# Two loads of the next batch's V, moved into an earlier chunk

## The chip, the cores and the metric

The kernel runs on one core of a Trainium2 chip. The metric is the time of one execution on the device in microseconds (us), as the median of several runs. Where a stretch of the run is meant, the times are from the first instruction of one profiled execution.

## What is computed

Eight batches of 3136 tokens. For each, scores of all tokens against all tokens from `z` (64 wide), a squared ReLU in place of a softmax, a sum over `v` (256 wide), and a product with `u`. Then 128 tokens of each batch, chosen by a gate, go through a two-layer network and replace their rows.

```python
scores = (1.0 / S) * np.matmul(z, z.transpose(0, 2, 1))
attn = np.maximum(scores, 0.0) ** 2
x = (u * np.matmul(attn, v)).astype(np.float32)
...
top_idx = np.argpartition(-s[b], capacity)[:capacity]      # s = x . w_gate
h = np.maximum(x[b, top_idx] @ w1, 0.0)
out[b, top_idx] = x[b, top_idx] + g[:, None] * (h @ w2)    # g = sigmoid(s[b, top_idx])
```

## The kernel before

Every matmul operand is kept as a high and a low part, and a product is made of three: high with high, high with low, low with high. In the profile `hi` and `lo` are the two parts of the squared scores, made by ACT (a cast) and by DVE or POOL (a subtraction).

A batch is worked through in seven chunks of columns: five of 512 (0 to 4), one of 256 (chunk 5) and one of 320 (chunk 6). A chunk has 13 slots: twelve with a pair of 128-row tiles of V each, and a last one for the 64 rows that are left. A slot is 12 matmuls into the chunk's two accumulator banks (line 561; in the last slot 4). A batch has 91 slots, and `k0` is the first slot of a batch.

The scores are symmetric. Where a chunk meets rows whose scores an earlier chunk has made, it doesn't compute them: the earlier chunk has transposed its squares (`aT`) and stored them to DRAM (`squares`, `squares_narrow`, `squares_last`), and `fetch` (line 382) brings them back into a buffer `qk`, of which there are three. Such slots are called old. In chunk 5 ten of twelve pairs are old, in chunk 6 eleven; one fetch serves two slots. For these, ACT makes `hi` from `qk` (line 423) and DVE or POOL makes `lo` (line 523). The work on scores runs `LEAD`, three, slots ahead of the matmuls that use it.

V of a batch comes from DRAM in thirteen steps. `stage_v` (line 284) loads four tiles of V (512 KB) into a buffer `vst` with four DMAs of 128 KB (line 293); there are two such buffers, which loads of weights and of stored squares (`fetch_own`, line 406) use too. `prep_v` (line 299) splits two of these tiles into high and low parts, on ACT (line 125) and POOL (line 126), into the buffers of V that the batch before leaves free in its last chunk.

When a chunk's last matmul is done, `finish` (line 600) multiplies its two banks with `u` on DVE (`ut`, line 607), which empties them. There are three banks for accumulators, so the next chunk's first bank is free at once and its second is free when the first `ut` is done. The first slot of a chunk works through its first bank, six matmuls, before it turns to the second (line 555).

All DMAs around here are issued by SP, one after the other in program order: fetches, loads of V, z and u, stores of squares and of the output (`out<-x`, line 626). Where one must wait for data or for a free buffer, all behind it wait.

The order is written out slot by slot. `plan` holds for each slot what is called ahead of its matmuls, in the order of the calls of `at_slot`. A fetch is planned `AHEAD`, seven, slots before its first use or as soon as a buffer is free (line 1352). `prep_v` for pair `g` stands at slot `k = k0 - 10 + 3 * g // 2` (line 1330), and the load of pairs `g` and `g + 1` three slots before it (line 1334). Loads are entered after the fetches (line 1366), so within a slot a fetch goes first. Stores that a slot's work has left go out after the next slot's matmuls are issued (line 1504).

Chunk 5 begins at slot `k0 - 26` and chunk 6 at slot `k0 - 13`. The first fetch for chunk 6 is so planned at slot 6 of chunk 5, the second at slot 9, and the first load of the next batch's V at slot 0 of chunk 6.

Of the kernel before, what the change touches and what calls it, by code (L numbers as in the profile page):

```python
# [88 lines left out]
def attention_then_routed_ffn(ctx: ExitStack, tc: tile.TileContext, zt, ut, v, wg, w1, w2, cst, cst16, keys, outs, at, cap):  # L89
# [141 lines left out]
    def stage_z(b, i, n=None, step=None, queues=(nc.sync, nc.sync)):  # L231
        a, w = part(i)
        n = n or w
        if n > CH or n != w:
            st = work.tile([P, CH // Q, GT * Q], F32, name="qk", tag="qk", bufs=NQ).rearrange("p f k -> p (f k)")
        else:
            st = stage.tile([P, CH], F32, name="zst", tag="zst", bufs=1)
        for h in range(2):
            queues[h].dma_start(st[h * 64 : h * 64 + 64, : step or n], zt[b, :, a : a + (step or n)])
        staged["z", b, i] = st  # L240

    def more_z(b, i, of):

        a, n = part(i)
        o = a - part(of)[0]
        for h in range(2):
            nc.sync.dma_start(staged["z", b, of][h * 64 : h * 64 + 64, o : o + n], zt[b, :, a : a + n])

    def prep_z(b, i, of=None, on=None, hi_on=None):

        of = i if of is None else of
        a, n = part(i)
        o = a - part(of)[0]
        m = min(n, NJ * P - a)
        src = staged["z", b, of][:, o : o + m].rearrange("p (f t a) -> p f t a", f=GT, a=Q)
        on = on or (nc.gpsimd.tensor_tensor if b else None)
        split(src, by_rows(ZH, a, m), by_rows(ZL, a, m), hi_on, lo_on=on)
        if m < n:
            split(staged["z", b, of][:, o + m : o + n], ZH[:, a + m : a + n], ZL[:, a + m : a + n], lo_on=on)
        spend(pool=0.65 + 0.0017 * n if b else 0.0)  # L260

    def bring_z(b, c):

        c0, w = CHUNKS[c]
        t = const.tile([P, CH], F32R, name="Z", tag="Z", bufs=2)[:, within(c)]
        for rows, z in ((slice(0, 64), ZH), (slice(64, P), ZL)):
            if b == 0 and c == 0:
                st = staged["z", 0, 0][rows]
                if z is ZH:
                    nc.scalar.copy(t[rows], st)  # L270
                else:
                    by_token = [x.rearrange("p (f t a) -> p f t a", t=GT, a=Q) for x in (t[rows], st)]
                    nc.vector.tensor_tensor(*by_token, by_rows(ZH, 0, CH)[rows].bitcast(F32), op=ALU.subtract)
            else:
                m = min(w, NJ * P - c0)
                nc.scalar.copy(
                    t[rows, :m].rearrange("p (f t a) -> p f t a", f=GT, a=Q), by_rows(z, c0, m)[rows].bitcast(F32)
                )
                if m < w:
                    nc.scalar.copy(t[rows, m:], z[rows, c0 + m : c0 + w].bitcast(F32))  # L280
                spend(act=0.1 + 0.001 * w)
        Z[b, c] = t

    def stage_v(b, g, queues=(nc.sync,) * GT):

        st = stage.tile([P, GT, D], F32, name="vst", tag="vst")
        if g < NJ // GT:
            tiles = GT if g < WHOLE else GT // 2
            for t in range(0, GT, tiles):
                for f in range(GT):  # L290
                    t0 = g * CH + t * P + f * tiles * Q
                    src = v[b, t0 : t0 + tiles * Q, :].rearrange("(t a) d -> a t d", a=Q)
                    queues[f].dma_start(st[f * Q : (f + 1) * Q, t : t + tiles], src)
        else:
            for h in range(2):
                nc.sync.dma_start(st[h * 64 : h * 64 + 64, 0, :], v[b, NJ * P :, :])
        staged["v", b, g] = st

    def prep_v(b, g, on=None):

        st = staged["v", b, g // 2][:, g % 2 * 2 :]
        n = 2 if 2 * g < NJ else 1
        if n == 2:
            t = vpool.tile([P, 2, NK, 2 * P], F32R, name="V", tag="V")
        else:
            t = vpool.tile([P, 2, NK, P], F32R, name="Vr", tag="Vr", bufs=1)
        src = st[:, :n].rearrange("p a d -> p (a d)").rearrange("p (f h i) -> p h f i", h=NK, i=Q)
        parts_of = [t[:, w].rearrange("p h (f i) -> p h f i", i=Q) for w in range(2)]
        lo_on, took = on or nc.gpsimd, {"dve": 1.0} if on else {"act": 0.6, "pool": 1.3}
        if not on and b == 0 and n == 2 and busy["pool"] + 1.3 > busy["dve"] + 0.6:  # L310
            lo_on, took = nc.vector, {"act": 0.6, "dve": 0.6}
        split(src, *parts_of, on and on.tensor_copy, lo_on.tensor_tensor)
        for q in range(n):
            V[b, 2 * g + q] = t[:, :, :, q * P : (q + 1) * P]
        spend(**took)
# [278 lines left out]
    def load_u(b, c):  # L594
        c0, w = CHUNKS[c]
        t = tail.tile([P, NK, CH], F32, name="ut", tag="ut", bufs=1)
        nc.sync.dma_start(t[:, :, :w], ut[b, :, :, c0 : c0 + w].rearrange("h p t -> p h t"))
        chunk[b, c] = t
# [700 lines left out]
    def at_slot(k, fn, act=0.0, dve=0.0):  # L1299
        if k < len(slots):  # L1300
            plan.setdefault(max(k, 0), []).append((fn, act, dve))

    def at_slots(k, load, use, act, dve=0.0, lead=2):

        at_slot(k, use, act, dve)
        loads.append((k - lead, load))
# [3 lines left out]
    for b in range(B):  # L1310
        k0 = b * per

        for i in range(NCH):
            if b == 0:
                k = (0, 0, 0, 1, 3, 5, 6)[i]
            elif i < WHOLE:
                k = k0 - per + (i + 1) * SLOTS + 7
            else:
                k = k0 - 1 + 4 * (i - WHOLE)
            use = lambda b=b, i=i: prep_z(b, i)  # L1320
            if b:
                at_slots(k, lambda b=b, i=i: stage_z(b, i), use, 0.6, lead=5 if i < WHOLE else 2)
            elif i > 2:
                at_slot(k, lambda i=i: prep_z(0, i, 1 if i < WHOLE else WHOLE), 0.6, 0.7)
                if i == WHOLE:
                    loads.append((2, lambda: stage_z(0, WHOLE, S + 64 - WHOLE * CH)))
                elif 3 < i < WHOLE:
                    loads.append((max(1, k - 3), lambda i=i: more_z(0, i, 1)))
        for g in range(NJ // 2 + 1):
            k = k0 - 10 + 3 * g // 2 if b else max(1, g - 3)  # L1330
            if b or g > 3:
                at_slot(k, lambda b=b, g=g: prep_v(b, g))
            if (b or g > 6) and g % 2 == 0:
                load = (k - (3 if b else 2), lambda b=b, g=g: stage_v(b, g // 2))
                if b or 2 * g < NJ:
                    loads.append(load)
                else:
                    at_slot(*load)
        for c in range(NCH):
            if b or c:  # L1340
                at_slot(k0 + c * SLOTS - LEAD - 4, lambda b=b, c=c: bring_z(b, c))
        for c in range(NCH):
            at_slot(k0 + c * SLOTS + 7, lambda b=b, c=c: load_u(b, c))
# [7 lines left out]
    for (b, c, g), ks in used.items():  # L1351
        k = max(ks[0] - AHEAD, room.popleft() - LEAD + 2)
# [6 lines left out]
    for i, (load, use) in enumerate(weight_tasks):  # L1359
        c, step = ((1, 11), (2, 4), (2, 10), (3, 4), (3, 10), (4, 4), (NCH + 1, 4), (NCH + 2, 4))[i]  # L1360
        k = c * SLOTS + step
# [232 lines left out]
```

## Time and profile before

| | |
|---|---|
| median of 3 runs | 2063.77 us (2062.52 to 2064.70) |
| the profiled execution | 2064.51 us, its span 2062.7 us |
| TensorE matmuls (PE) busy | 2046.9 us |
| VectorE (DVE) busy | 1531.1 us |
| POOL (GpSimd) busy | 1356.5 us |
| ScalarE (ACT) busy | 1291.0 us |
| granted clock of TensorE | 1.00 of full speed in the stretches looked at |
| moved by DMA | 415.52 MB, mean 201 GB/s |

Idle time of an engine is listed with what ended it; TensorE's is the one that makes the run longer. The ends of matmuls are modelled in the profile, so the distance between the starts of two matmuls tells more than the end of one. In a timeline a row merges like instructions that follow each other (x4), and brackets hold the idle time of the engine before it and what ended that.

### The profile page before, as it was taken

What the parts mean: (1) busy time and instruction counts of PE and PEld (TensorE: products, weight loads), DVE (VectorE), ACT (ScalarE), POOL (GpSimd) and SP (SyncE); (2) the same over time, 40 slices, a digit from 0 to 9 for tenths busy, and PEclk for the clock granted to TensorE, in tenths of its full rate; (3) what the DMA queues carried; (4) which work ended last, traced back from release to release, by engine and by line L of the source; (5) the groups of instructions that cost most, each with busy time, mean ns of one, the idle gap of its engine ahead of it and who ended that gap; (6) DMA issues with size and microseconds to landing.
All of it is one profiled execution on the core that took longest, in us unless ns stands there. A gap on an engine that the chain in (4) does not pass through costs nothing.

```text
span 2062.7 us, 31660 instructions
## 1 busy us (share of the span) xinstructions
PE 2046.9 (99%) x10280; PEld 1735.4 (84%) x10280; DVE 1531.1 (74%) x2667; ACT 1291.0 (63%) x1629; POOL 1356.5 (66%) x728
## 2 busy tenths in 40 slices
PE   9999999999999999999999999999999999999999
PEld 6888988889888898888988889888898888888788
DVE  7676678856788667875678757887578876787776
ACT  7665577655775467664676546765477655775543
POOL 6766587655876568764677647875578755665653
PEclk9999999999999999999999999999999999999999
DMA  6788767886668875787767877678676786666862
GB/s 198 209 235 227 212 188 207 238 227 187 197 185 232 214 209 176 198 237 206 207 184 194 237 202 218 183 194 239 191 222 187 193 197 182 206 190 164 216 173 95
DMA packets 442758, 415.52 MB, mean 201 GB/s; under 512 B 133792, under 2 KB 374880, under 8 KB 439520
## 3 DMA queue, kind: packets, MB, share of 16 engines
q1 hardware_dynamic: 441456, 411.01, 70.8%
q0 software_dynamic: 768, 2.10, 0.3%
q8 instruction: 80, 1.31, 0.3%
q14 instruction: 86, 0.70, 0.1%
q10 hardware_dynamic: 368, 0.39, 0.1%
HBM read 238.78 MB, written 174.60 MB: 200 GB/s over the span
## 4 chain that ended last, share of the span: by engine, by line
PE 78%; DVE 8%; DMA 4%; issue 3%; ACT 3%; SPq 2%; POOL 2%; POOLq 0%; DVEq 0%; ACTq 0%
PE acc L561 65%; PE sc L445 11%; DVE aT L488 2%; DVE a L467 2%; DMA qk<-squares_narrow 1%; DMA squares<-aT 1%; POOL lo L523 1%; ACT a L455 1%; ACT hi L456 1%; DVE lo L523 1%; PE h L1223 1%; PE y L1267 1%; DMA vst<-in_v 1%; DVE base L773 0%; DVE ut L607 0%
## 5 line engine op out<-in xcount | busy, mean ns | idle before, releaser
L561 PE MATMUL acc<-hi,V 128*128 128x512 f32 (+2 forms) x5376 | 1213.2, 364 | 4.8 <-DVE ut L607 2.3
L523 POOL TENSOR_TENSOR lo<-a,hi 128x1024 fp32r<-128x1024 f32 (+2 forms) x326 | 719.4, 2209 | 556.4 <-DVE a L467 443.0
L561 PEld LDWEIGHTS acc<-hi,V 128*128 128x128 f32 x5376 | 928.3, 188 | 162.4 <-DVE ut L607 8.4
L561 PE MATMUL acc<-lo,V 128*128 128x512 f32 (+2 forms) x2688 | 661.5, 362 | 1.5 <-POOL lo L523 1.4
L455 ACT ACTIVATE a<-sc 128x1024 f32<-128x1024 f32 (+4 forms) x401 | 358.5, 894 | 444.3 <-PE sc L445 419.4
L561 PEld LDWEIGHTS acc<-lo,V 128*128 128x128 f32 x2688 | 468.7, 188 | 77.8 <-POOL lo L523 4.5
L467 DVE TENSOR_TENSOR a<-sc,a 128x1024 f32<-128x1024 f32 (+5 forms) x306 | 307.5, 1005 | 244.3 <-ACT hi L456 220.0
L423 ACT CAST hi<-qk 128x1024 fp32r<-128x1024 f32 (+2 forms) x327 | 279.0, 860 | 223.0 <-PE acc L561 188.5
L488 DVE STREAM_TRANSPOSE aT<-a 128x512 f32<-128x512 f32 (+3 forms) x541 | 349.6, 681 | 75.5 <-ACT a L461 55.1
L456 ACT ACTIVATE hi<-a 128x1024 fp32r<-128x1024 f32 (+4 forms) x401 | 372.3, 928 | 24.7 <-PE acc L561 2.2
L523 DVE TENSOR_TENSOR lo<-qk,hi 128x1024 fp32r<-128x1024 f32 (+2 forms) x220 | 321.8, 1473 | 85.1 <-ACT hi L423 83.1
L445 PE MATMUL sc<-Z,ZH 128*128 128x512 f32 (+2 forms) x746 | 274.3, 372 | 2.5 <-DVE a L467 2.1
L445 PE MATMUL sc<-Z,ZL 128*128 128x512 f32 (+2 forms) x746 | 273.1, 370 | 0.0
L523 POOL TENSOR_TENSOR lo<-qk,hi 128x1024 fp32r<-128x1024 f32 (+2 forms) x107 | 209.5, 1960 | 50.2 <-ACT hi L423 41.1
L445 PEld LDWEIGHTS sc<-Z,ZH 128*128 128x128 f32 x746 | 140.0, 188 | 31.9 <-DVE a L467 6.0
L445 PEld LDWEIGHTS sc<-Z,ZL 128*128 128x128 f32 x746 | 140.1, 188 | 24.8 <-DVE ZL L126 0.4
L126 POOL TENSOR_TENSOR V<-vst,V 128x512 fp32r<-128x512 f32 x92 | 137.1, 1496 | 30.3 <-ACT V L125 27.2
L628 POOL TENSOR_TENSOR ut<-x,w_run 128x1024 f32<-128x1024 f32 (+2 forms) x52 | 125.6, 2416 | 30.3 <-DVE x L619 29.3
L461 ACT ACTIVATE a<-a 128x1024 f32<-128x1024 f32 x93 | 98.8, 1062 | 2.9
L126 POOL TENSOR_TENSOR ZL<-zst,ZH 128x512 fp32r<-128x512 f32 (+2 forms) x56 | 83.5, 1496 | 2.4 <-ACT ZH L125 2.1
L125 ACT CAST V<-vst 128x512 fp32r<-128x512 f32 x95 | 57.9, 609 | 36.6 <-DMA vst<-in_v 36.6
L607 DVE SCALAR_TENSOR_TENSOR ut<-acc,ut 128x512 f32<-128x512 f32 (+2 forms) x112 | 63.9, 612 | 19.5 <-PE acc L561 19.2
(187 smaller groups left out, 1081.2 us busy)
## 6 DMA issues: line engine op xcount, KB each, us to landing
squares<-aT SPq DMA_DIRECT2D x160, 512.0 KB
qk<-squares SPq DMA_DIRECT2D x320, 256.0 KB
squares_narrow<-aT SPq DMA_DIRECT2D x320, 128.0 KB
qk<-squares_narrow SPq DMA_DIRECT2D x80, 512.0 KB
out<-x SPq DMA_DIRECT2D x162, 128.0 KB
ut<-in_ut SPq DMA_DIRECT2D x40, 512.0 KB
vst<-in_v SPq DMA_DIRECT2D x158, 128.0 KB
squares_own<-aT SPq DMA_DIRECT2D x39, 256.0 KB
```

The source lines that it names most:

```text
L126: (lo_on or nc.vector.tensor_tensor)(lo, src, hi.bitcast(F32), op=ALU.subtract)
L423: nc.scalar.copy(by(hi), src)
L445: nc.tensor.matmul(ps[:, q], z[:, j * P : (j + 1) * P], mov, start=z is ZH, stop=z is ZL)
L455: nc.scalar.activation(a, ps[:, :n], AF.Relu)
L456: nc.scalar.activation(pieces[0][0](hi), pieces[0][1], AF.Square)
L461: nc.scalar.activation(a, a, AF.Square)
L467: square = lambda: nc.vector.tensor_tensor(a[rows], of[rows, :n], a[rows], op=ALU.mult)
L488: nc.vector.transpose(to, a[rows, q].rearrange("p (m t a) -> p m t a", m=GT, a=Q))
L523: on.tensor_tensor(view(lo), src, view(hi).bitcast(F32), op=ALU.subtract)
L561: nc.tensor.matmul(ac[h], w, mov, start=first and h not in started, stop=stop)
L607: nc.vector.scalar_tensor_tensor(xT[:, h, :w], acc[b, c][h], SCALE * SCALE, xT[:, h, :w], op0=ALU.mult, op1=ALU.mult)
L628: nc.gpsimd.tensor_tensor(wx, runs, consts["wg_run"].rearrange("p (o r) -> p o r", o=1).broadcast_to([P, NB, RUN]), op=ALU.mult,)
```

## The change

In the plan of V's loads, for every batch but the first, the load of pairs 0 and 1 moves from slot `k0 - 13` to `k0 - 22`, and that of pairs 2 and 3 from `k0 - 10` to `k0 - 17`. These are slots 4 and 9 of the 256-column chunk, nine and seven slots sooner. All other loads keep their slots (`13 - 3 * g // 2` is the old distance), and `prep_v` keeps its own.

```diff
-                load = (k - (3 if b else 2), lambda b=b, g=g: stage_v(b, g // 2))
+                load = (k0 - {0: 22, 2: 17}.get(g, 13 - 3 * g // 2) if b else k - 2, lambda b=b, g=g: stage_v(b, g // 2))
```

## Rows read from the trace of the kernel before

**Rows 1.** The page, part 1: busy us (share of the span), instructions.

```profile
PE 2046.9 (99%) x10280; PEld 1735.4 (84%) x10280; DVE 1531.1 (74%) x2667; ACT 1291.0 (63%) x1629; POOL 1356.5 (66%) x728
```

**Rows 2.** Waits of PE, whole run: us in total, times, longest us.

```profile
PE acc L561 <- DVE ut L607: 2.3, 5, 0.6
PE acc L561 <- ACT hi L423: 2.1, 2, 1.2
```

**Rows 3.** Waits of all engines, whole run: ACT's for loads of V.

```profile
ACT V L125 <- DMA vst<-in_v: 36.6, 21, 4.9
```

**Rows 4.** Stretches, seams 1, 2, 4: length, busy us by engine, clock, DMA share, GB/s.

```profile
233.24:258.66 25.42, 24.84 (x164) 24.07 (x163) 17.24 (x22) 17.49 (x27) 14.79 (x10) 1.00 0.76 211
488.33:514.91 26.58, 25.39 (x164) 24.13 (x163) 15.74 (x21) 17.16 (x26) 15.14 (x10) 1.00 0.72 196
...
997.13:1023.34 26.21, 25.31 (x164) 24.13 (x163) 15.79 (x21) 17.36 (x26) 15.19 (x10) 1.00 0.72 201
```

**Rows 5.** Timeline of PE, first slot of chunk 6, seams 1 and 2: start, length.

```profile
233.82 0.45 PE L561 MATMUL acc<-lo,V 128*128 128x320 f32 x2
234.85 0.86 PE L561 MATMUL acc<-hi,V 128*128 128x320 f32 x4 [0.58 <-DVE ut L607]
...
488.91 0.45 PE L561 MATMUL acc<-lo,V 128*128 128x320 f32 x2
489.20 0.84 PE L561 MATMUL acc<-hi,V 128*128 128x320 f32 x4
```

**Rows 6.** Timeline of ACT around seams 1, 2 and 4.

```profile
232.02 1.35 ACT L423 CAST hi<-qk 128x640 fp32r<-128x640 f32 x2 [1.90 <-DVE aT L488]
...
238.99 0.73 ACT L423 CAST hi<-qk 128x640 fp32r<-128x640 f32 x1 [1.06 <-PE acc L561]
...
486.33 0.73 ACT L423 CAST hi<-qk 128x640 fp32r<-128x640 f32 x1 [1.12 <-DMA qk<-squares_narrow]
...
498.98 0.62 ACT L125 CAST V<-vst 128x512 fp32r<-128x512 f32 x1 [4.92 <-DMA vst<-in_v]
...
995.15 0.73 ACT L423 CAST hi<-qk 128x640 fp32r<-128x640 f32 x1 [1.14 <-DMA qk<-squares_narrow]
```

**Rows 7.** Timeline of DVE at seam 1, around the chunk's finishing step.

```profile
232.78 1.56 DVE L523 TENSOR_TENSOR lo<-qk,hi 128x640 fp32r<-128x640 f32 x2 [0.78 <-ACT hi L423]
234.37 0.76 DVE L607 SCALAR_TENSOR_TENSOR ut<-acc,ut 128x256 f32<-128x256 f32 x2
```

**Rows 8.** Timeline of SP's issues, seam 1; the last row is seam 2.

```profile
223.14 0.52 SPq L399 DMA_DIRECT2D qk<-squares_narrow  x1
223.76 2.73 SPq L626 DMA_DIRECT2D out<-x  x4
226.59 1.15 SPq L399 DMA_DIRECT2D qk<-squares_narrow  x1
227.79 0.52 SPq L402 DMA_DIRECT2D qk<-squares_narrow  x1
...
229.35 0.49 SPq L402 DMA_DIRECT2D qk<-squares_narrow  x1
232.03 0.80 SPq L503 DMA_DIRECT2D squares_last<-aT  x2
...
233.36 0.52 SPq L402 DMA_DIRECT2D qk<-squares_narrow  x1
...
235.33 2.02 SPq L293 DMA_DIRECT2D vst<-in_v  x4
...
482.10 0.54 SPq L402 DMA_DIRECT2D qk<-squares_narrow  x1
```

**Rows 9.** Stretches of the DMA burst, seams 2 and 1: columns as in Rows 4.

```profile
484.60:488.33 3.73, 3.73 (x35) 3.73 (x34) 2.96 (x5) 1.97 (x4) 1.84 (x2) 1.00 0.98 332
226.50:234.80 8.30, 7.77 (x66) 7.51 (x64) 5.60 (x9) 4.82 (x9) 4.29 (x3) 1.00 1.06 281
```

**Rows 10.** Timeline of POOL: the last reader of a `vst` buffer before seam 1.

```profile
197.52 2.29 POOL L523 TENSOR_TENSOR lo<-vst,hi 128x512 fp32r<-128x512 f32 x1
```

## Prediction

> **What bounds the kernel now.** I read the busy table first. TensorE is busy for 2046.9 us of a 2062.7 us span [rows 1], so a change to loads can only act through the few microseconds in which TensorE waits. The list of TensorE's own waits names them [rows 2]: five waits for the finishing step of a chunk (`ut`, line 607) and two for the hi casts of ACT (line 423). Then I asked for ACT's waits: it stands idle 36.6 us in 21 waits for loads of V [rows 3]. That is the wait that the change goes for, and the question is how much of it reaches TensorE.
>
> It is read from the stage where it happens. A batch ends with a 256-column chunk and a 320-column chunk; I call the passage from one batch to the next a seam, and there are seven. For seams 1, 2 and 4 I took the stretch from the first matmul of the 320-column chunk to the first of the next batch [rows 4]. The work in each is the same, yet they last 25.42, 26.58 and 26.21 us. Two different waits make the differences.
>
> The first is V. In seam 2 ACT waits 4.92 us for the first load of V, and of TensorE's two waits for casts, 2.1 us in all and 1.2 the longest, one follows there [rows 2, 6]. ACT works three slots ahead of TensorE, so the shorter V waits of the other seams are covered: TensorE waits for these casts only twice in the run [rows 2].
>
> The second is the finishing step. In the first slot of the 320-column chunk the second accumulator bank must wait for `ut` on DVE. In seam 2 there is no wait: two lo matmuls at 488.91, the next group at 489.20, 0.29 us of work. In seam 1 the same steps stand at 233.82 and 234.85: 1.03 us, so 0.74 are lost (0.58 in the row, whose ends are modelled) [rows 5]. Why is `ut` late in seam 1? DVE runs two lo subtractions before it, from 232.78, and these wait for ACT's casts of the same data [rows 7]; the first of these casts begins at 232.02 [rows 6]. From cast to `ut` it is 2.35 us (232.02 to 234.37), from `ut` to the matmul 0.48. That gives a formula: stall = cast begin − chunk begin + 1.96. It gives 0.74 for seam 1 (232.02 − 233.24 + 1.96), −0.04 for seam 2 (486.33 − 488.33 + 1.96) and −0.02 for seam 4 (995.15 − 997.13 + 1.96) [rows 4, 6]. So the stall follows the cast one for one, and even the two seams without a stall have no slack: 0.04 and 0.02 us.
>
> What does that cast wait for? The fetch of the first old squares of the 320-column chunk: ACT's idle time ends on `qk<-squares_narrow` in seams 2 and 4 [rows 6]. In seam 1 a transpose of DVE is named, but the cast comes 4.23 us after the fetch's second DMA was issued (227.79), as it does in seam 2 (482.10 to 486.33) [rows 6, 8]. So **the fetch issued at 226.59 decides when TensorE gets into the 320-column chunk**, and it stands in a burst: from 226.50 to 234.80 the 16 DMA engines are busy for 1.06 of the time, that is, always [rows 9].
>
> **The change, part by part.** It adds no instruction. In each of seven seams it moves four DMAs (512 KB) nine slots forward, to slot 4 of the 256-column chunk, and four more seven slots forward (17 stands where 10 was), to slot 9. ACT, DVE, POOL and TensorE keep their programs; only SP's queue is reordered, and SP issues strictly in that order.
>
> *Taken away: the V waits.* V is issued some 9 us sooner (behind the stores that end at 226.5, not at 235.33) [rows 8], and its buffer has long been free: the last reader, POOL's `lo<-vst`, is done at 199.8 [rows 10]. On TensorE this is worth what seams 2 and 4 lose by it. The chunk without any stall is 25.42 − 0.74 = 24.68 us, so 26.58 − 24.68 = 1.90 and 26.21 − 24.68 = 1.53 [rows 4], together **3.4 us**. The rest of ACT's wait is hidden now and worth nothing.
>
> *First load, moved past the critical fetch.* The fetch of 226.59 is planned for slot 6 of the 256-column chunk (seven ahead of its first use). The moved load stands at slot 4, so it enters SP's queue behind the fetch of 223.14 and the stores of out that follow it, and just ahead of the fetch of 226.59; before, it came after it, at 235.33 [rows 8]. Its price can be seen in two ways. By issue: its four DMAs hold SP for 2.02 us (row of 235.33), and SP has no gap there to absorb them. By transfer: 524 KB at the 281 GB/s of the busy stretch are 1.87 us, at the 332 GB/s of seam 2's best stretch 1.58 us [rows 9]. I take 1.75 us, between the two transfer prices, since the engines are full, with 1.5 and 2.2 as ends. A gain is excluded here: nothing that stands ahead of the fetch is taken away. A price of nothing is the first rival. By the formula each seam pays it in full, 7 × 1.75 = **12.25 us**; in seams 2 and 4 the slack takes off 0.06 in all.
>
> The Trainium skill (DMA: Bandwidth & Descriptors, Specifications) gives 435 GB/s as the ceiling of the fabric; an estimate by it is 1.2 us for the 512 KB, and 8.4 − 3.4 = 5.0 us over seven seams. No row of this stretch reaches that rate [rows 9], so the rows decide.
>
> *Second load.* It goes behind the second fetch of the 320-column chunk, whose last DMA is the row of 229.35, and SP stands from 229.84 until 232.03 anyway, so most of its issue lies in that gap [rows 8]. Behind it comes the third fetch (its second DMA at 233.36). Its cast, at 238.99, waits for TensorE and not for data [rows 6]; it begins 5.6 us after that DMA [rows 8], where 4.23 were enough above. That leaves 1.4 us, and TensorE is itself later by 1.75. Both loads' 3.5 us of transfer use this up and little more, and three slots of lead stand behind it: I take nothing. If that cover is gone, 0.5 us a seam, 3.5 us in all, comes on top.
>
> **Sum.** The profiled execution took 2064.51 us, its span 2062.7 and 1.8 around it. 2064.5 − 3.4 + 12.25 = 2073.3. That run lies 0.74 above the median of 2063.77, so against the median **2072.6 us**, +0.43%. With 1.5 and 2.2 us a seam it is 2070.9 to 2075.8, and with the second load's 3.5 us on the upper end 2079.
>
> **Rivals.**
> 1. *The fetch is not delayed* (not slower). The engines take the load beside the fetch, or the stores of out drain so slowly that its place makes no difference; what remains is the gain of 3.4 us: 2060.4, within 0.2%. For it speaks that the engines move at most 332 GB/s here and might have room; against it, that they are busy all the time [rows 9]. It decides where the added delay is under half a us a seam (7 × 0.5 = 3.5). 12%. Beside it stands a rule of the Trainium skill (DMA: Bandwidth & Descriptors, Rules for kernel authors), to issue a DMA early and wait for it late so that its cost overlaps: this would be its result.
> 2. *Half a delay.* The load's transfer overlaps with the tail of the stores, and 0.85 us reach the cast. 7 × 0.85 − 3.4 = 2.5: 2066.3, no difference that can be measured. 10%.
> 3. *A second stall.* The third fetch is late by more than its cover, over 0.9 us more a seam: above 2078.5. 4%.
> 4. *More gained.* The reordering lets the critical fetch land earlier than now, so that the bank stalls go as well: 2.3 us in rows 2, about 2.9 at seam 1's ratio of 0.74 to 0.58. 2063.8 − 3.4 − 2.9 = 2057.5. Nothing in the queue speaks for it. 3%.
>
> **How the numbers follow.** The forecast has 71%. About 0.2%, 4.1 us, is what a measurement can tell from no change. Slower by more than that (above 2067.9): the forecast, the third rival and a little of the second, 0.77. Faster (below 2059.6): rival 4 and a tail of the first, 0.05. Same: 0.18. The range runs from 2065 to 2078.5: the forecast's bounds and the half delay; rivals 1, 3 and 4 are left out (19%).
>
> **What would show it.** If I am right: the 256-column chunk keeps its length; in the first slot of the 320-column chunk TensorE waits for `ut` L607 in all seven seams, 1.7 to 2.6 us by the matmuls' starts (0 in seam 2 and 0.74 in seam 1 now); ACT's first cast for it begins about 1.75 us later against the chunk's beginning (−2.0 and −1.2 us now); ACT's wait for `vst` falls from 36.6 us to under 10; TensorE's two waits for ACT's `hi` are gone; the 320-column stretches last 26.4 to 27.4 us. The forecast is wrong if the first cast keeps its time, if SP issues the fetch ahead of the load, or if the stall grows in a few seams alone.

## The result, and the profile after

The changed kernel takes 2077.16 us in the median (2074.91 to 2081.23), the kernel before, in the same comparison, 2062.57 us (2060.63 to 2064.70): a ratio of 1.0074, with a 95% interval from 1.0064 to 1.0083. It is slower by 0.74%, inside the range of the prediction, on the side that it gave 0.77, and 4.6 us above its point of 2072.6 us. As a change it is 14.6 us between these medians, where 8.85 were forecast, and 10.4 us between the two profiled spans. The profiled execution took 2074.91 us with a span of 2073.1 us; it lies 2.25 us under the median.

Instructions and their order are the same on TensorE, ACT and POOL, and on DVE but for one pair of neighbours near the end of the run. TensorE's busy time, in part 1 of the page, is 5.0 us more than in [rows 1]:

```profile
PE 2051.9 (99%) x10280; PEld 1737.5 (84%) x10280; DVE 1539.9 (74%) x2667; ACT 1290.2 (62%) x1629; POOL 1366.6 (66%) x728
```

The list of waits, whole run (us in total, times, longest us), answers [rows 2, 3]:

```profile
ACT hi L423 <- DMA qk<-squares_narrow: 41.8, 19, 4.5
...
ACT V L125 <- DMA vst<-in_v: 13.4, 7, 2.6
...
PE acc L561 <- ACT hi L423: 6.3, 7, 2.3
PE acc L561 <- DVE ut L607: 4.4, 7, 0.6
```

The wait for V fell from 36.6 to 13.4 us, and seven waits are left where there were 21. In its place stands the wait for old squares, which was 11.2 us in 9 waits. TensorE now waits for ACT and for `ut` once in each of the seven seams.

The queue that the change reorders is SP's. Its issues at seam 1, as in [rows 8]:

```profile
223.60 0.52 SPq L399 DMA_DIRECT2D qk<-squares_narrow  x1
224.22 3.05 SPq L626 DMA_DIRECT2D out<-x  x4
227.32 2.74 SPq L293 DMA_DIRECT2D vst<-in_v  x4
230.17 0.38 SPq L399 DMA_DIRECT2D qk<-squares_narrow  x1
230.60 0.50 SPq L402 DMA_DIRECT2D qk<-squares_narrow  x1
...
232.69 2.49 SPq L293 DMA_DIRECT2D vst<-in_v  x4
```

The first load stands between the stores of `out` and the critical fetch, as the prediction had it, and the fetch is issued at 230.17 instead of 226.59. ACT's timeline shows what follows, at seams 1, 2 and 4 (idle time and what ended it in brackets; compare [rows 6]):

```profile
235.29 1.35 ACT L423 CAST hi<-qk 128x640 fp32r<-128x640 f32 x2 [4.51 <-DMA qk<-squares_narrow]
...
492.76 1.36 ACT L423 CAST hi<-qk 128x640 fp32r<-128x640 f32 x2 [2.91 <-DMA qk<-squares_narrow]
...
501.72 0.61 ACT L125 CAST V<-vst 128x512 fp32r<-128x512 f32 x1
...
1002.68 1.35 ACT L423 CAST hi<-qk 128x640 fp32r<-128x640 f32 x2 [2.91 <-DMA qk<-squares_narrow]
```

The cast of V at 501.72 waits for nothing any more; it is the one that waited 4.92 us. The casts for chunk 6 all wait for the fetch. TensorE's timeline shows the price, in the first slot of chunk 6 at seams 1 and 2, as in [rows 5]:

```profile
236.07 0.85 PE L561 MATMUL acc<-hi,V 128*128 128x320 f32 x4 [2.34 <-ACT hi L423]
236.93 0.56 PE L561 MATMUL acc<-lo,V 128*128 128x320 f32 x2
238.12 1.29 PE L561 MATMUL acc<-hi,V 128*128 128x320 f32 x4 [0.63 <-DVE ut L607]
...
493.54 0.85 PE L561 MATMUL acc<-hi,V 128*128 128x320 f32 x4 [0.41 <-ACT hi L423]
...
495.59 0.86 PE L561 MATMUL acc<-hi,V 128*128 128x320 f32 x4 [0.63 <-DVE ut L607]
```

There are two stalls in place of one. The chunk's first matmul itself waits for the cast, and the second bank then waits for `ut`, as before. The stretches of chunk 5 and chunk 6 at seams 1 and 2 (length, busy us by engine, clock, DMA share, GB/s), and a piece of seam 1:

```profile
214.95:236.07 21.12, 18.78 (x164) 18.52 (x162) 10.48 (x17) 10.41 (x21) 13.16 (x9) 1.00 0.69 202
236.07:263.48 27.41, 26.77 (x162) 25.74 (x163) 16.70 (x22) 17.93 (x27) 15.68 (x10) 0.94 0.63 176
474.36:493.54 19.18, 18.78 (x163) 18.52 (x161) 11.51 (x17) 10.53 (x21) 13.27 (x9) 1.00 0.73 209
493.54:519.44 25.90, 25.25 (x162) 24.19 (x163) 19.22 (x22) 17.64 (x27) 16.18 (x10) 1.00 0.67 196
...
238.30:241.70 3.40, 3.40 (x14) 3.40 (x15) 0.83 (x2) 0.72 (x1) 2.43 (x2) 0.50 0.79 200
```

Chunk 5 lasted 18.62 us before (469.71 to 488.33 in seam 2); it lasts 21.12 and 19.18 now, since the wait ahead of chunk 6's first matmul falls into it. The last line is new: for 3.40 us after the stalls of seam 1 the granted clock of TensorE was 0.50, its lower level of 1.2 GHz. In the other six seams of this execution it stayed at the upper level.

**Where the time went.** For each seam I took the time from chunk 5's first matmul to the next batch's first. Without any stall it is 18.62 + 24.68 = 43.30 us, and what lies above it is lost. Over the seven seams that was 6.6 us before and is 18.0 us now: 11.4 more. The rest of the run is 1.1 us shorter, and the span grew by 10.4 us. The prediction's formula (stall = cast begin − chunk begin + 1.96), with the stall-free 18.62 us for the length of chunk 5, splits the sums:

| us, seven seams | before | after | change | predicted |
|---|---|---|---|---|
| stall by the formula | 3.1 | 15.7 | +12.6 | +12.25 |
| lost to V (seams 2 and 4) | 3.4 | 0 | −3.4 | −3.4 |
| seam 1 beyond the formula (half clock) | 0 | 1.55 | +1.55 | – |
| seams 4 and 7 beyond the formula | 0 | 0.7 | +0.7 | – |

### The profile page after: what moved, and what is told of

Its sections match the earlier page's. It is cut to its first block, busy times and chain, and to the rows that moved or that the text cites. A ratio compares the mean times of both kernels' runs of the same rounds, so it can differ in the third digit from the quotient of the medians.

```text
span 2073.1 us, 31632 instructions
## 1 busy us (share of the span) xinstructions
PE 2051.9 (99%) x10280; PEld 1737.5 (84%) x10280; DVE 1539.9 (74%) x2667; ACT 1290.2 (62%) x1629; POOL 1366.6 (66%) x728
## 3 DMA queue, kind: packets, MB, share of 16 engines
q8 instruction: 80, 1.31, 0.3%
## 4 chain that ended last, share of the span: by engine, by line
PE 82%; DVE 5%; DMA 3%; issue 3%; ACT 3%; SPq 2%; POOL 1%; POOLq 0%; ACTq 0%; DVEq 0%
PE acc L561 68%; PE sc L445 12%; DMA qk<-squares_narrow 2%; DVE a L467 1%; ACT a L455 1%; ACT hi L456 1%; DVE aT L488 1%; DVE lo L523 1%; SPq L293 1%; PE h L1223 1%; POOL lo L523 1%; PE y L1267 1%; POOL V L126 1%; DMA vst<-in_v 1%; SPq L626 0%
## 5 line engine op out<-in xcount | busy, mean ns | idle before, releaser
L561 PE MATMUL acc<-hi,V 128*128 128x512 f32 (+2 forms) x5376 | 1215.1, 364 | 11.2 <-ACT hi L423 6.3
L523 DVE TENSOR_TENSOR lo<-qk,hi 128x1024 fp32r<-128x1024 f32 (+2 forms) x220 | 330.2, 1510 | 83.8 <-ACT hi L423 81.8
L126 POOL TENSOR_TENSOR V<-vst,V 128x512 fp32r<-128x512 f32 x92 | 145.0, 1586 | 9.5 <-ACT V L125 9.2
L619 DVE STREAM_TRANSPOSE x<-ut 128x512 f32<-128x512 f32 (+2 forms) x110 | 67.1, 618 | 0.2
```

What stands on the lines that cost most here:

```text
L126: (lo_on or nc.vector.tensor_tensor)(lo, src, hi.bitcast(F32), op=ALU.subtract)
L523: on.tensor_tensor(view(lo), src, view(hi).bitcast(F32), op=ALU.subtract)
L561: nc.tensor.matmul(ac[h], w, mov, start=first and h not in started, stop=stop)
L619: nc.vector.transpose(x[:, :, h, :], xT[:, h, :w].rearrange("p (f q) -> p f q", q=Q))
```

## The experiments

Several theories stand against each other. **A**, the prediction's: the first load delays the critical fetch. **B**: the harm is the second load's, which stands ahead of the third fetch. **C**: not the order does the harm, but 512 KB more in chunk 5, wherever they stand. **The clock**: part of the loss is that TensorE falls to half clock after a stall. And within A there are two views, which the prediction named and chose between: **by issue** (SP is held by four more DMAs) and **by transfer** (the engines move 512 KB more). Each run is compared with the kernel before on the same chip, at 2062.9 to 2063.7 us. Where an edit changes only the table of slots in the changed line, its diff shows the table alone.

The same two numbers are taken from each profile: when the second DMA of the critical fetch is issued, and when ACT's first cast for chunk 6 begins. Both are counted from chunk 5's first matmul and are means over the seven seams, worked out from the rows of SP and ACT. They are brought together here, and the sections refer to them.

| kernel | what stands ahead of the fetch | fetch issued | cast begins | issue to cast |
|---|---|---|---|---|
| before | – | 12.64 | 17.10 | 4.46 |
| after | 4 DMAs, 512 KB | 14.65 | 18.91 | 4.26 |
| e10 | 4 DMAs, 2 KB | 14.93 | 18.90 | 3.97 |
| e11 | 1 DMA, 512 KB | 13.44 | 18.65 | 5.21 |
| e4 | 8 DMAs, 1 MB | 16.71 | 21.48 | 4.77 |
| e7 | 8 DMAs, 1 MB, seven and six slots ahead of it | 13.36 | 17.85 | 4.49 |
| e2 | 512 KB right behind the fetch | 12.79 | 17.86 | 5.07 |
| e13 | 512 KB behind the fetch and `u` | 12.64 | 17.34 | 4.70 |
| e14 | 512 KB behind the second fetch | 12.63 | 16.83 | 4.20 |
| e12 | none on SP; both loads issued by ACT | 14.54 | 20.10 | 5.56 |

**e1, the first load alone.** The second goes back to its old place.

```diff
-{0: 22, 2: 17}
+{0: 22}
```

> Only the first load of V stands in slot 4 of the 256-column chunk; the second is back in chunk 6, where the kernel before has it. Theory A (the first load stands ahead of the critical fetch in SP's queue and makes it late): the first cast of chunk 6 begins 1.3 to 2.0 us later against the chunk's nominal begin than before in every seam, TensorE waits there in all seven, and the time is 9 to 15 us over before, as in the changed kernel. Theory B (the second load does the harm, through the third fetch): no stall at chunk 6's beginning beyond those of before, time 2 to 4 us under before.

Measured: 2079.74 us, ratio 1.0074 [1.0061, 1.0088], much the same as the whole change; it is 16.0 us over before, just above the expected 9 to 15. The cast begins at 19.42 on average, 0.5 us later than in the changed kernel, which was not traced; its profile has the half clock at two seams. The first load does the harm by itself; B falls for this change.

**e2, the first load just behind the critical fetch**, ahead of the load of `u`; the second at its old place.

```diff
-{0: 22, 2: 17}
+{0: 20}
```

> Only the first load is moved, to slot 6: in SP's queue right behind the fetch that it stood ahead of, and still ahead of the load of u. The second load is where the kernel before has it. Theory A: the fetch lands as before, the waits of seams 2 and 4 for V (3.4 us) go, and the load of u lands 1.6 to 2 us later, which reaches the finishing step by 0.5 us a seam at most; time 3.4 under before to equal. Theory C (not the order: 512 KB more in the burst of the 256-column chunk do the harm wherever they stand): the first cast is still over 1 us late and the time 5 us or more over before.

Measured: 2066.89 us, ratio 1.0018 [1.0008, 1.0027]. The same 512 KB, one place later in the queue, cost 3.2 us and not the 16.0 of e1. Most of the harm comes from the place, so A holds and C does not. It isn't free, though equal at most was expected: the fetch is issued as before (12.79), but takes 0.6 us longer to its cast, presumably since the load's transfer runs beside it. `u` comes later too, and in six seams DVE's `ut` waits for it, up to 0.41 us. No wait of TensorE in the first slots hangs on V any more, and this gain is given back.

**e3, both loads behind the fetch and `u`.**

```diff
-{0: 22, 2: 17}
+{0: 19, 2: 17}
```

> First load in slot 7, behind the fetch and the load of u; second load in slot 9 as in the changed kernel. Theory A: no stall that before has not, V's waits in seams 2 and 4 gone, 3.4 us under before. Theory B (second load): loss remains, 5 us or more over before. Theory C (contention): loss remains, 10 us or more over before.

Measured: 2071.44 us, ratio 1.0039 [1.0025, 1.0052]. The casts for chunk 6 are not late (16.87), and yet the kernel is slower. ACT's timeline at seam 3, and one of the waits of the run:

```profile
753.03 0.73 ACT L423 CAST hi<-qk 128x640 fp32r<-128x640 f32 x1 [3.62 <-DMA qk<-squares_narrow]
...
765.35 0.62 ACT L125 CAST V<-vst 128x512 fp32r<-128x512 f32 x1 [4.08 <-DMA vst<-in_v]
```

```profile
PE sc L445 <- DVE a L467: 7.1, 16, 1.2
```

Now the third fetch is late: its second DMA goes out 22.29 us from chunk 5's start on average, 18.73 before, and the cast at 753.03 waits for it. What follows is late down the chain, POOL's parts of V among it, which free the buffer for the third load of V; ACT waits 4.08 us for that load, and TensorE in the end for the scores of the next batch (7.1 us in 16 waits; 2.1 in four before). With the first load alone at this place (e13 below) the third fetch goes out at 19.59 and the time is 2062.89 us, so the second load makes the difference, and B's mechanism is real. In the changed kernel the third fetch goes out later still, at 22.99, and TensorE doesn't wait for it; that its own delay covers this is the likely reason.

**e4, both loads ahead of the fetch**: the dose of the first is doubled.

```diff
-{0: 22, 2: 17}
+{0: 22, 2: 22}
```

> Both loads in slot 4, eight DMAs (1 MB) ahead of the critical fetch: the dose doubled. Theory A: the first cast is 3.2 to 4 us late instead of 1.8, so 7 x 3.5 - 3.4 = 21 us over before; with the halved clock that the trace of the changed kernel shows behind the longest stall (0.50 for 3.4 us after 2.3 us of idling, worth 1.6 us), in most seams, 28 to 33 us over before. If what stands ahead of the fetch did not count by its size, the time would be that of the changed kernel, 12 to 15 us over.

Measured: 2104.19 us, ratio 1.0192 [1.0176, 1.0208]. The fetch is issued 4.07 us later than before and the cast begins 4.38 us later: 2.4 times the changed kernel's 1.81. The time is 40 us longer, though, where 28 to 33 were expected, and 7 × 4.38 less the 3.4 of V gives 27. The stretches show the rest: at six of the seven seams the clock is halved for 6.80 us, at the seventh for 3.4. For seam 2:

```profile
499.70:506.50 6.80, 6.17 (x24) 6.08 (x24) 2.51 (x6) 2.06 (x3) 3.06 (x2) 0.50 0.62 209
```

**e5 and e8, TensorE kept busy in the stall.** To test the clock, matmuls are put ahead of chunk 6's first slot, of 320 columns, on data that lies ready; their result is overwritten. e5 is the changed kernel with 8 of them, e8 is e4 with 20.

```diff
+        if first and c == NCH - 1 and b < B - 1:
+            for _ in range(8):
+                nc.tensor.matmul(ac[0], ZH[:, :P], ZH[:, : CHUNKS[c][1]], start=True, stop=True)
```

> The changed kernel with eight matmuls of 320 columns, whose result is overwritten, at the head of chunk 6 of every batch but the last, where TensorE idles now. They need nothing that is waited for and last 1.1 us, less than the 1.75 us that each seam idles. Clock theory (part of the loss over the predicted size is TensorE's halved clock behind the long idle times, seen at seam 1 only in the profiled run, in more seams in others): no stretch of clock 0.50 at a seam, time 1.5 to 5 us under the changed kernel, 2072 to 2075. Without it: the time of the changed kernel, 2077 or a little more.

> Both loads in slot 4, as in the run with the doubled dose, and twenty such matmuls (2.7 us) at the head of chunk 6, which idles 3 to 4.6 us there. Clock theory: the stretches of 0.50 (44 us in all at the seams) go, and 10 to 13 us of the 40 us over before with them: 2091 to 2095. Without it: 2104 as without the filling, or more.

Measured: e5 2075.72 us, ratio 1.0067 [1.0053, 1.0081]; e8 2090.32 us, ratio 1.0129 [1.0113, 1.0144]. In e8 the same stretch of seam 2 is at full clock:

```profile
499.70:506.50 6.80, 6.17 (x42) 6.18 (x43) 4.68 (x8) 3.52 (x6) 3.08 (x2) 1.00 0.49 158
```

The cast of e8 begins at 21.24, 0.24 from e4's, and the kernel is 13.9 us faster with 140 matmuls more. Up to 1.7 us of this is the earlier cast (7 × 0.24). Two seams of e8 still have 3.40 us of half clock, the first of them here:

```profile
240.80:244.20 3.40, 3.40 (x15) 3.40 (x14) 0.41 (x1) 1.05 (x2) 2.85 (x2) 0.50 0.64 196
```

So in e4 some 12 us of the loss, three tenths, went with the half clock of the other seams. In e5 the half clock of seam 1 is gone too, and what seam 1 lost beyond the formula (1.55 us) with it; the matmuls added cost something in the seams with short stalls, and the time is 1.4 us under the changed kernel's, inside the intervals of both. For the change itself the clock is a small part, and its size is not settled by the times.

**e7, both loads in front of chunk 5's queue**: at the last slot of chunk 4 and the first of chunk 5, seven and six slots ahead of the fetch.

```diff
-{0: 22, 2: 17}
+{0: 27, 2: 26}
```

> Both loads earlier still: the first in the last slot of chunk 4, the second in slot 0 of chunk 5, where SP waits 2.8 and 3.4 us for a buffer and for a transpose, and where the DMA engines stand at 0.44 of their time. Theory A (place in the queue decides): no fetch is late, V's waits of seams 2 and 4 go, 3.4 us under before, 2059 to 2061. If the harm came with any move of V out of chunk 6: over before by 3 us or more, as with the loads behind the fetch.

Measured: 2064.85 us, ratio 1.0006 [0.9997, 1.0015], no change that can be measured. ACT waits for none of the first four casts of V. But the fetch is issued 0.72 us later and the cast begins 0.75 us later: the queue seems to be pushed back even from there, and what V gave is given back.

**e10, the four DMAs without their bytes.** The kernel before, with four DMAs of 512 bytes each at the place of the moved load; what they bring is not used. V is loaded where it was.

```diff
+    crumbs = const.tile([P, 4], F32, name="crumbs")
+    def tiny(b):
+        for f in range(GT):
+            nc.sync.dma_start(crumbs[f * Q : (f + 1) * Q], v[b, f * Q : (f + 1) * Q, :4])
...
+        if b:
+            loads.append((k0 - 22, lambda b=b: tiny(b)))
```

> The kernel before, with four tiny DMAs (2 KB in all) in slot 4 of the 256-column chunk, where the changed kernel has the first load of V; V's loads stay in chunk 6. If the fetch is late because SP is held by four more issues (2 us): the first cast is 1.5 to 2 us later in every seam, time 12 us over before or more. If it is late because 512 KB stand ahead of it in the DMA engines: the cast at most 0.5 us later, time 0 to 3 us over before.

Measured: 2085.96 us, ratio 1.0112 [1.0097, 1.0128]. The queue of SP and the cast at seam 1:

```profile
228.01 2.81 SPq L303 DMA_DIRECT2D crumbs<-in_v  x4
230.94 0.39 SPq L405 DMA_DIRECT2D qk<-squares_narrow  x1
231.37 0.51 SPq L408 DMA_DIRECT2D qk<-squares_narrow  x1
```

```profile
235.44 1.35 ACT L429 CAST hi<-qk 128x640 fp32r<-128x640 f32 x2 [3.81 <-DMA qk<-squares_narrow]
```

2 KB hold SP for 2.81 us, as 512 KB do in the changed kernel (2.74), and the cast is as late (18.90 and 18.91). No transfer is needed for most of the delay. That the two casts agree so well is in part luck: e10's fetch goes out 0.28 us later than the changed kernel's, which was not traced, and its way to the cast, without the bytes beside it, is 0.29 us shorter. The time as a whole is not to be compared: the V waits stay, two seams have the half clock, and outside the seams the run is 8.9 us longer than before. The matmuls that make scores are slower in this kernel, by 5 and 4 ns on average (397 and 394 ns; 392 and 390 before, 602 of each, 5.4 us together); why a small tile more does that was not traced.

**e11, the bytes in one DMA.** The kernel before, with a single DMA of 512 KB at that place, into the buffer that the load fills again at its old place.

```diff
+    def whole_v(b):
+        st = first[b, 0] = stage.tile([P, GT, D], F32, name="vst", tag="vst")
+        nc.sync.dma_start(st, v[b, : GT * P, :].rearrange("(t p) d -> p t d", p=P))
...
+            loads.append((k0 - 22, lambda b=b: whole_v(b)))
```

> Counterpart of the four tiny loads: the kernel before, and at slot 4 of chunk 5 one single DMA of 512 KB into the buffer of the first load, ahead of the critical fetch; the four DMAs of the load follow at their old place, so V's data is asked for twice. Issue theory (each DMA ahead of the fetch holds it by the 0.43 us of its own issue, whatever it carries): the cast for chunk 6 begins 17.5 to 17.7 us into the seam, 0.4 to 0.6 later than before, and the time is 2064 to 2068. Transfer theory (the 512 KB themselves hold the fetch): 18.7 to 18.9 us, as in the changed kernel, and 2073 to 2077, as the waits for V stay.

Measured: 2071.96 us, ratio 1.0039 [1.0026, 1.0053]. SP and the cast at seam 1:

```profile
226.78 1.73 SPq L288 DMA_DIRECT2D vst<-in_v  x1
228.62 0.44 SPq L407 DMA_DIRECT2D qk<-squares_narrow  x1
```

```profile
233.82 1.36 ACT L431 CAST hi<-qk 128x640 fp32r<-128x640 f32 x2 [3.17 <-DMA qk<-squares_narrow]
```

The cast begins 1.55 us later than before, just under the transfer view's 1.58 to 1.87, and not the half a us that one issue would cost; the time lies 1 us under the range expected for it. Of the 1.55, 0.80 us is later issue and 0.75 us a longer way from issue to cast. So either alone delays the cast: four issues without bytes by 1.80 us, the bytes with a single issue by 1.55. Together they cost 1.81 and not 3.35. This fits a transfer that is hidden under the issuing, where the longer of the two, here the issuing, decides; the overlap itself was inferred from these sums.

**e12, the loads issued by ACT.** The change as it is, but ACT issues the two loads.

```diff
-lambda b=b, g=g: stage_v(b, g // 2))
+lambda b=b, g=g: stage_v(b, g // 2, (nc.scalar if b and g < 4 else nc.sync,) * GT))
```

> The change as it is, but its two loads are issued by ACT instead of SP, at the same slots. SP's queue is that of the kernel before, with eight DMAs fewer. Issue theory: the cast for chunk 6 is not late (at most 17.1 us on average), the waits for V are gone, ACT pays some 8 x 0.5 us of issuing per seam where it has idle time: 2058 to 2063. Transfer theory: the same bytes are asked for ahead of the fetch, the cast is 1.5 to 1.8 late and the time 2070 to 2077. Third case: ACT's issuing itself makes its casts late; then the cast begins late without an idle gap ahead of it that ends on a DMA.

Measured: 2084.82 us, ratio 1.0092 [1.0076, 1.0108]. ACT's timeline at seam 1:

```profile
220.46 3.27 ACTq L293 DMA_DIRECT2D vst<-in_v  x4
223.85 1.14 ACT L423 CAST hi<-qk 128x512 fp32r<-128x512 f32 x2 [2.79 <-DMA vst<-in_v]
```

ACT stands 2.79 us in its own issuing, which lasts until 223.73, and TensorE waits for the `lo` that hangs on those casts (nine waits for POOL's `lo`, 3.7 us; three, 1.4 before). The fetch on SP is no earlier for it: it goes out at 14.54, and its cast begins at 20.10, later than in the changed kernel; three seams have the half clock. Another issuing engine is no way out here. The Trainium skill (DMA: Bandwidth & Descriptors, Issuing engines are not separate DMA queues) says that DMAs started by different engines run on the same 16 DMA engines, and that only the time on the sequencer is saved. The run agrees with the first half: with the loads issued by ACT beside it, the fetch takes 5.56 us from issue to cast, and 4.46 before. It doesn't show the saving, as the fetch's issue was held on SP all the same. In the trace SP issues it at 229.32, just after the landing, at 229.25, of an earlier store that used the same semaphore; that this is the cause was not tested.

**e13 and e14, the first load alone, behind the critical fetch.** e13 puts it behind the fetch and `u`, e14 behind the second fetch, where SP stands idle for 2.2 us [rows 8].

```diff
-{0: 22, 2: 17}
+{0: 19}
```

and e14:

```diff
-{0: 22, 2: 17}
+{0: 17}
```

> Only the first load moves, to slot 7 of chunk 5, behind the critical fetch and the load of u; the second stays at its old place, behind the third fetch. If lateness of the critical fetch and of the third fetch were all the harm, both are gone: casts at 16.5 to 17.2 us, none of the waits on the third fetch that moving both behind u showed, the two waits for V of seams 2 and 4 gone: 2060 to 2063. If the early first load only hands the wait on to the second or third load of V, ACT waits there, and the time is 2063 to 2067.

> Only the first load moves, to slot 9 of chunk 5: behind the second fetch, where SP stands for 2.2 us anyway; the second load keeps its old place. What moving it behind u still cost is the transfer beside the critical fetch (cast 0.24 us later on average, 17.34). Here it starts about 1.5 us later. If that competition was the cost, the casts are back at 17.0 to 17.2, and as the waits for V ahead of the first casts are gone too, the time is 2059 to 2062, 0.1 to 0.2% under the kernel before. Rival: the third fetch, which the load now stands ahead of, lands late (its cover is 1.4 us), ACT waits for it in the second pair of slots and the time is 2063 to 2067.

Measured: e13 2062.89 us, ratio 0.9999 [0.9990, 1.0008]; e14 2065.24 us, ratio 1.0012 [1.0003, 1.0021]. TensorE's waits, of e13 and then of e14:

```profile
PE acc L561 <- DVE ut L607: 2.5, 5, 0.6
```

```profile
PE acc L561 <- ACT hi L423: 3.1, 4, 1.8
...
PE acc L561 <- DVE ut L607: 0.6, 1, 0.6
```

In e13 the waits for V are gone from TensorE, and the cast is 0.24 us later, 7 × 0.24 = 1.7 us. In its profile the seams lose 5.2 us, 1.4 less than before, which the times don't show. In e14 the casts are back in time (16.83) and `ut` is waited for once. But the third fetch, which now stands behind the load, goes out at 21.32 instead of 18.73, and the wait for V is handed on to the second load, although from chunk 5's start that is issued no later on average than before. At seam 2:

```profile
502.26 0.62 ACT L125 CAST V<-vst 128x512 fp32r<-128x512 f32 x1 [2.91 <-DMA vst<-in_v]
```

TensorE's four waits for ACT, up to 1.8 us, each follow such a cast. No place that was tried is faster than the kernel before.

## Why the prediction was right, and where it wasn't

**The chain was right.** The load stands ahead of the fetch, the fetch sets the cast, the cast sets TensorE's entry into chunk 6, in every seam and one for one. The formula, taken from seam 1 before, gives after's seams 2, 3, 5 and 6 within 0.03 us (for seam 2: 18.41 − 18.62 + 1.96 = 1.75 against 1.78 lost).

**The price was right, its reason wrong.** I had two prices for the first load, 2.02 us by issue and 1.58 to 1.87 by transfer, and took 1.75 by transfer "since the engines are full". The cast is 1.81 us later on average, and 7 × 1.81 less the little that was free is the 12.6 us of the table. But e10 has as long a delay with 2 KB. The fetch's second DMA is issued 2.01 us later, which is the price by issue, and its way to the cast is 0.20 us shorter, presumably because the engines have drained meanwhile. In one DMA the same bytes cost 1.55 (e11), 0.80 of it by later issue; beside four issues they add little. That the choice did no harm is luck: the two prices happen to be alike. Cut into sixteen DMAs, the same bytes would cost some 16 × 0.48 = 7.7 us of issuing (an estimate from the distance of two issues behind the first, 228.67 and 229.15 in the changed kernel; not run), and I would still have said 1.75.

**The V gain was right**, 3.4 us: neither of the two waits on TensorE is left. The wait of ACT that remains is 13.4 us, where I said under 10: it is all for the third load of V, which the change doesn't move and which I hadn't looked at. It seems to cost TensorE little: seams 4 and 7, where it is longest (2.65 and 2.46 us), lose 0.7 us in all beyond the formula, at the scores of the next batch.

**Chunk 5 did not keep its length.** I let the whole stall fall on the wait for `ut`, where it stood in [rows 5]. That wait can't grow beyond what lies between the chunk's first six matmuls and `ut`; a cast that is later still holds up the first matmul. So the `ut` wait is 0.90 us by the starts in each seam (236.93 to 238.12 at seam 1, less 0.29 of work) and not the 1.7 to 2.6 that I named; 0.28 more go by between the chunk's first matmul and its first with `lo`, which comes at 0.86 us (236.93 at seam 1) instead of 0.58; and the rest, 0.57 us in seam 2, stands ahead of the chunk. The sum is the same, the place isn't. The stretches of chunk 6 that I named as a sign, 26.4 to 27.4 us, did not come: seam 1 has 27.41 at half clock, the other six 25.86 to 26.32.

**The second load costs nothing, but by one half of the cover that I named.** I counted 1.4 us of cover and TensorE's own delay. e3 takes the delay away and keeps the load's place, and TensorE waits at once: the third fetch is 3.56 us late there, far over 1.4. What covered the load was the harm done by the first one.

**The clock was missing.** The sum let TensorE run at full clock throughout. At seam 1 it didn't: that was 1.55 us of the change, in one seam; in e4, with twice the dose, some 12 us or more.

**From the sum to the time.** The profiled execution was forecast at 2073.3 and took 2074.91: +0.3 from the cast's 12.6, +2.3 beyond the formula, −1.1 outside the seams make 1.5 of the 1.6. The rest of the 4.6 us against the median is that before's profiled run lay 0.74 above its median, and after's lies 2.25 under it. The clock may be part of this as well: the two executions of the changed kernel with a mean granted clock of 0.999 took 2074.91 and 2076.09 us, the four with 0.998 took 2076.65 to 2081.23, as if the clock had fallen at more seams there; this isn't shown, since only the profiled execution has a trace. A slip in the range did no harm: with the second load's 3.5 us the forecast reached 2079.3, and the range ended at 2078.5.

Of the rivals, the first and second (no delay, half a delay) are excluded by the cast's 1.81 us, the third (a second stall) by e1, and the fourth by SP's queue.

## What to carry to other kernels

A load that is moved forward in an in-order queue is paid by what it passes: look up the next transfer behind its new place that an engine waits for, and price the move by its issue time as well as by its transfer time; here the larger of the two came out. In this kernel, where the queue is full around a seam, every place that was tried handed the wait on: behind the fetch (e2), behind `u` (e13) and behind the second fetch (e14) another consumer came late each time, and the 3.4 us at stake never showed in the time. A stall term that was measured where it was small may split when it grows; sum over both chunks, and ask what the engine's clock does after it.

## What the runs showed of the hardware

**Four tiny DMAs hold the queue like four large ones.** On SP each takes about 0.43 us: 0.42 in the median for 512 bytes (28 DMAs of e10) and 0.43 for 128 KB (the loads of V in the changed kernel). The first DMA behind the stores of `out` takes longer at seam 1, whatever it is: 1.15 us for a fetch before, 1.31 for 128 KB in the changed kernel, 1.42 for 512 bytes in e10, 1.73 for 512 KB in one (e11). What it is held by stays open.

**The clock after a stall.** In the changed kernel, seam 1: TensorE stood 2.34 and 0.63 us, with six matmuls between, and from 238.30 the granted clock was 0.50 for 3.40 us. TensorE's timeline, eight matmuls at the lower level and eight at the upper:

```profile
239.74 2.23 PE L561 MATMUL acc<-hi,V 128*128 128x320 f32 x8
...
242.39 1.33 PE L561 MATMUL acc<-hi,V 128*128 128x320 f32 x8
```

In e4, at seam 1, TensorE stood 4.41 us:

```profile
237.94 1.44 PE L561 MATMUL acc<-hi,V 128*128 128x320 f32 x4 [4.41 <-ACT hi L423]
```

and the clock was 0.50 for 6.80 us, from 236.9 on, before TensorE went on. So in e4 one us of delay on the fetch cost more than one us of the run.
